# Attention and gated-MLP gradients on one core: where dV^T, dK^T, K^T and V^T are turned

## The chip, the core and the metric

The kernel runs on one core of a Trainium2 chip. The metric is the device time of one execution in microseconds (us). The engines named below are TensorE (PE, with its weight loads PEld), VectorE (DVE), ScalarE (ACT), GpSimd (POOL) and SyncE (SP). Here SP issues the DMA transposes, which turn 2-byte data on the way through the crossbar into SBUF, and POOL issues nearly all plain DMAs. Each of the two has one in-order queue of instructions, and the transfers of both run on the same 16 DMA engines. In the profile the transfers issued by SP are q1 ("hardware_dynamic") and those issued by POOL are q0 ("software_dynamic").

## The reference, cut to what matters

The forward pass and the gradients of eight of its inputs are computed, in bf16, with S = 2048 rows, D = 576, H = 32 heads of Dh = 128 (so HD = 4096) and F = 4608:

```
xn = layernorm(x)
q  = xn @ wq                              # per head [2048, 128]
p  = softmax(q k^T / sqrt(128))           # per head [2048, 2048]
s  = concat_heads(p v) @ wo
g  = silu((sigmoid(xn @ w_gate) * (xn @ w_up)) @ w_down)
out = x + s * g
grads of x, k_cache, v_cache, wq, wo, w_gate, w_up, w_down for a given grad_out
```

Two of the gradients matter here: out_2 is dK and out_3 is dV, both [32, 2048, 128], 512 KB for each head.

## The kernel before, in words

The work goes through stages. The times are those of the profiled execution.

1. **MLP forward** (to about 485 us): g, u, the products with w_down, and the gradient that enters attention. At its end K^T of head 0 is made by PE transposes (`prep_kt`, line 553).
2. **Attention** (about 485 to 3615 us): 32 heads. A head has 32 *slots*, one for each of its 16 query tiles in phase 1 and one for each in phase 2. Phase 1 (`main1`, line 640) makes the scores of one query tile, [128, 2048], on PE (line 631), ACT takes the exponential into a bf16 *slab* (line 649), and SP turns the slab by DMA transpose (`transpose_slab`, line 625) into a tile of the pool `wpt`, named PT. Phase 2 (`main2`, line 697) makes dP on PE (line 701), ACT and DVE make dS in the same slab (lines 704 to 708), and SP turns it again (dST). Five slots (`SKEW`) after its slab was made, `tail1` or `tail2` multiplies the turned slab with V or K (line 678), 16 matmuls for each slab.
3. **Output projection** (to about 3764 us, lines 905 to 962): needs all heads' outputs from scratch, turned by `load_oT` (line 582).
4. **MLP weight gradients** (about 3764 to 4339 us, lines 1010 to 1066): 18 blocks of 256 columns. A block has 16 `dh` products with their DVE and ACT work, and then six accumulations over 16 row tiles (`accumulate`, line 977): two for d w_down, two for d w_up, two for d w_gate. The last four are turned by SP (line 1063). Loads of the next block, stores of du and dg, and stores of gradients go through POOL.
5. **Attention weight gradients** (about 4339 to 4590 us, lines 1102 to 1127): eight groups of four heads. A head has one accumulation for d wo and one for d wq, which SP turns (line 1120). At a group's start POOL issues the 2 MB loads `load_on` and `load_dq` for the next group. After every second head SP also turns one of ten pieces of w_up and w_gate (128 x 4608, `load_T_rows`, line 63) for the last stage.
6. **dx** (to the end): accumulations over 104 blocks (line 1159), fed by DMA transposes (line 1098).

Within attention, the heads' side work is laid out by `plan` (line 784): `put(slot, cols, fn)` hangs a piece of work into a slot, with its cost in PE columns. The four pieces that matter:

- `prep_kt` (line 795): 16 PE transposes of K of the *next* head in slot 12 of phase 2 (`NTH + 4`), through PSUM, with two ACT copies of 128 x 1024 (line 40).
- `prep_vt` (line 807): 16 PE transposes of V in slot 11 of phase 1, with two DVE copies (line 42). Both go through `pe_transpose_blocks` (line 146).
- `Partial` for dV^T: two halves over the query tiles. The second half ends in slot 7 of phase 2 and writes its sum, [128, 2048], into the buffer of K^T, which is free by then (line 749). Then SP turns that buffer into the tile `kvn` (line 752) and POOL stores it to out_3 (line 753).
- `Partial` for dK^T: the same, one phase later. It ends in slot 7 of the next head's phase 1, uses the buffer of V^T, and goes to out_2.

K^T and V^T of the next use may be written only when those buffers are free again. In attention the order of the instructions on each engine is made by the framework's scheduler from this program order and the dependencies. In stages 3 to 6 the order on SP and POOL is the program's own (`manual_schedule`, line 881).

Of the kernel before, what the change touches and what calls it, by code (L numbers as in the profile page):

```python
# [13 lines left out]
P = 128  # L14
# [52 lines left out]
def kernel(  # L67
# [41 lines left out]
    gd_d = dram.tile([2, P], f32, name="gd_d")  # L109
    on2_d = dram.tile([S, HD], bf, name="on2_d")  # L110
    dq2_d = dram.tile([S, HD], bf, name="dq2_d")

    pers = ctx.enter_context(tc.tile_pool(name="pers", bufs=1))
    ident = pers.tile([P, P], bf, name="ident")
# [476 lines left out]
    def attention(fast):  # L591
        with ExitStack() as es:
# [1 line left out]
                return es.enter_context(tc.tile_pool(name=("f_" if fast else "g_") + name, bufs=bufs, **kw))  # L594
            slabp = pool("slab", SLABS)
            wsneg = None if fast else pool("wsneg", 3)
            wpt = pool("wpt", 7 if fast else 4)
            wt, stg = pool("wt", 2), pool("stg", 2)
            stat, hstat = pool("stat", 8), pool("hstat", 2)
            ps_big = pool("ps_big", 2, space=PSUM)  # L600
# [7 lines left out]
            acc_box[0] = acc_alloc  # L608
            warm = stat.tile([P, 1], f32, name="warm")
            nc.scalar.activation(warm[:], eps_t[:], AF.Exp)  # L610

            def start_head(h):
                hs = heads_pre[h] if h == 0 else new_head(h)
# [107 lines left out]

            class Partial:

                def __init__(self, hs, lo, hi, nat, part, turned, out_dram, eng, factor=1.0):
                    self.lo, self.hi, self.nat, self.factor = lo, hi, nat, factor
                    self.part = part[:].rearrange("p t d -> p (t d)")
                    self.turned, self.out_dram, self.eng = turned, out_dram, eng
                    self.n = 0
                    self.slabs = hs.slabs

                def step(self):
                    chunk, j = divmod(self.n, SUB)
                    self.n += 1
                    cs = slice(chunk * CH, (chunk + 1) * CH)
                    if j == 0:
                        self.acc = acc_tile()[:].rearrange("p a b -> p (a b)")[:, :CH]
                    m = self.hi - self.lo
                    for qt in range(self.lo + m * j // SUB, self.lo + m * (j + 1) // SUB):
                        nc.tensor.matmul(self.acc, lhsT=self.nat[:, qt, :], rhs=self.slabs[qt][:, cs],  # L739
                                         start=(qt == self.lo), stop=(qt == self.hi - 1))  # L740
                    if j < SUB - 1:
                        return
                    if self.out_dram is None:
                        if self.factor == 1.0:
                            alt.copy(self.part[:, cs], self.acc, eng=self.eng)
                        else:
                            alt.scaled(self.part[:, cs], self.acc, self.factor, eng=self.eng)
                        return
                    nc.vector.scalar_tensor_tensor(self.turned[:, cs], self.acc, self.factor, self.part[:, cs], op0=ALU.mult, op1=ALU.add)
                    if chunk == NCH - 1:  # L750
                        kvn = stg.tile([P, NT, P], bf, name="kvn", bufs=1)
                        nc.sync.dma_start_transpose(kvn[:], self.turned)
                        nc.gpsimd.dma_start(self.out_dram.rearrange("(p t) d -> p t d", t=NT), kvn[:])

            def part_tile():
                return stg.tile([P, NT, P], f32, name="part", tag="part", bufs=1)
# [27 lines left out]
            def plan(h):  # L784
                b1, b2 = 2 * NT * h, 2 * NT * h + NT
                hd = lambda: heads[h]
                pl = b2 - 2 * NT if h else None
                if h:
                    put(pl, 0, lambda: heads.__setitem__(h, start_head(h)))
                    for c in range(4):  # L790
                        put(pl + q(c), 0, lambda c=c: load_k(hd(), c, 4))
                        put(pl + q(skew + 3 + c), 0, lambda c=c: load_v(hd(), c, 4))
                    put(pl + q(4), 0, lambda: load_wo(hd()))
                    put(pl + q(5), 0, lambda: load_wq(hd()))
                    put(pl + q(NTH + 4), NT * P, lambda: prep_kt(hd()))
                    put(pl + q(skew + 4), DT * P, lambda: prep_wot(hd()))
                    for sc in range(NSC):
                        put(pl + q(skew + 4 + 2 * sc), DT * CH, lambda sc=sc: prep_qt(hd(), sc))
                for qt in range(NT):
                    put(b1 + qt + skew, NT * P // 2, lambda qt=qt: tail1(hd(), qt, 0))  # L800
                    put(b1 + qt + skew, NT * P // 2, lambda qt=qt: tail1(hd(), qt, 1))
                for sc in range(NSC):
                    put(b1 + q(sc), DT * CH, lambda sc=sc: prep_dot(hd(), sc))
                    put(b1 + q(sc + 1), nb * P, lambda sc=sc: prep_don(hd(), sc))
                for qt in range(NT):
                    put(b1 + max(qt + 1, q(2 + qt // nb)), 0, lambda qt=qt: scale_don(hd(), qt))
                put(b1 + q(NTH + 3), NT * P, lambda: prep_vt(hd()))
                put(b1 + q(NTH + 2), NT * P, lambda: prep_qn(hd()))
                for qt in range(NT):
                    put(max(b1 + qt + 1, b1 + NT - 4 + qt // 2 if qt < NTH else b1 + NT + qt), 0, lambda qt=qt: scale_qn(hd(), qt))  # L810
                put(b2 + 1, 0, lambda: post1(hd()))
                parts = {}

                def first(key, rhs, lo, hi, eng, factor=1.0):
                    parts[key] = part_tile()
                    return Partial(hd(), lo, hi, rhs, parts[key], None, None, eng, factor)
                spread(b1 + NTH, lambda: first("v", hd().dOn, 0, NTH, "v"))
                spread(b2, lambda: Partial(hd(), NTH, NT, hd().dOn, parts["v"], hd().KT, out_3[0, h], None))
                spread(b2 + NTH, lambda: first("k", hd().Qn, 0, NTH, "s", SCALE))
                spread(b2 + NT, lambda: Partial(hd(), NTH, NT, hd().Qn, parts["k"], VT[:], out_2[0, h], None, SCALE))  # L820
                for qt in range(NT):
                    put(b2 + qt + skew, NT * P // 2, lambda qt=qt: tail2(hd(), qt, 0))
                    put(b2 + qt + skew, NT * P // 2, lambda qt=qt: tail2(hd(), qt, 1))
# [56 lines left out]
    with late("pc") as pc, late("pcw") as pcw, late("pcf") as pcf, \  # L880
# [126 lines left out]
        def load_dq(dq_, hg):  # L1007
            nc.gpsimd.dma_start(dq_, rows_view(dq2_d, hg * HG * P, HG * P))

        with late("b1r", 2) as dblk, late("b1l") as ldp, late("b1t", 3) as tmpp, late("b1o", 2) as outp, \  # L1010
                late("b1ps", 4, space=PSUM) as ps, late("b1pa", 2, space=PSUM) as psa:
            ah1 = ldp.tile([P, 2, NT, FB], bf, name="ah1")
# [3 lines left out]
            for fb in range(NFB):  # L1016
# [11 lines left out]
                if fb == NFB - 1:  # L1028
                    if NFB % 2:
                        dqb0_late = True  # L1030
                    else:
                        dqb0_late = False
                        load_dq(dqb0, 0)
                for st in range(NT):
                    srows = slice(st * P, (st + 1) * P)
                    dh = ps.tile([P, FB], f32, name="dh")
# [11 lines left out]
                if fb == NFB - 1:  # L1048
                    nc.gpsimd.dma_start(ds_all, rows_view(ds_d, 0, D))
                    load_on(onb0, 0)  # L1050
                for fl in range(FB // P):
                    dwd = outp.tile([P, D], bf, name="dwd")
                    accumulate(psa, h_blk, doB, slice(fl * P, (fl + 1) * P), dwd, "acc")
                    r0 = fb * FB + fl * P
                    nc.gpsimd.dma_start(out_8[r0:r0 + P, :], dwd[:])
                for (blk_, out_, nm) in ((du_blk, out_7, "dwu"), (dg_blk, out_6, "dwg")):
                    stg_ = outp.tile([P, DT, FB], bf, name=nm)
                    for fl in range(FB // P):
# [43 lines left out]
        with late("c2w") as wp, late("c2b") as blk, late("c2s", 2) as sb, late("c2ps", 4, space=PSUM) as ps:  # L1102
# [3 lines left out]
            for hg in range(NHG):  # L1106
# [6 lines left out]
                for hl in range(HG):  # L1113
                    h = hg * HG + hl
                    lcols = slice(hl * P, (hl + 1) * P)
                    dwo = sb.tile([P, D], bf, name="dwo")
                    accumulate(ps, onb, ds_all, lcols, dwo, "acc")
                    nc.gpsimd.dma_start(out_5[h * P:(h + 1) * P, :], dwo[:])
                    accumulate(ps, dqb, xn_all, lcols, dqTs[h % 2], "acc")
                    nc.sync.dma_start_transpose(dwq[:, :, lcols], dqTs[h % 2][:])  # L1120
                    if h % gap == gap - 1 and wT_pieces:
                        load_T_rows(nc, *wT_pieces.pop(0))
                    if hg == NHG - 1 and hl < len(cf_pre) and NHG % 2 == 0:
                        chunks[hl] = load_chunk(hl)
                store_T(out_4, cols, dwq)
            while wT_pieces:
                load_T_rows(nc, *wT_pieces.pop(0))

        with late("c4s", 2) as sb, late("c4cf") as chp, late("c4ps", 2, space=PSUM) as ps:
            wqT_sb = wd_flat[:, :H * D].rearrange("p (h d) -> p h d", d=D)  # L1130
# [104 lines left out]
```

## Time and profile before

| what | us |
|---|---|
| median of 9 runs | 5011.94 (5004.31 to 5024.34) |
| profiled execution | 5016.16 |
| its span | 5014.4 |
| PE busy | 4899.3 (98%) |
| DVE busy, ACT busy | 2574.7, 2573.5 (51% each) |
| crossbar queue q1: share of 16 DMA engines' span | 76.9% for 732.94 MB |
| plain queue q0: the same | 20.2% for 323.04 MB |
| `kvn` stores, 512 KB each: issue to landing, median | 5.2, 64 times |
| PT and dST transposes, 512 KB each: issue to landing, median | 4.8 and 5.1, 512 times each |

A busy PE is one whose matmuls follow each other; a matmul's own duration (219 ns for 128 columns) is longer than the pitch at which such matmuls follow, since they are pipelined. The share of a DMA queue counts the time that its packets took, so it can pass 100% when packets of two transfers overlap on an engine.

### The profile page before, as it was taken

The numbers are of one execution on the slowest core, as the hardware profiler recorded it, in microseconds if no ns is written. First come the engines' busy times: TensorE is split into PE (matmuls) and PEld (weight loads), VectorE is DVE, ScalarE is ACT, GpSimd is POOL, SyncE is SP. The second block draws the span as 40 slices with busy tenths as digits, with TensorE's granted clock in tenths as the row PEclk, the third lists the DMA queues.
The fourth block names the chain that finished last, engine by engine and source line by source line (L and its number), as shares of the span: only waits on it lengthen the run. The fifth ranks groups of instructions, "written<-read, shape, count | busy, mean of one in ns | idle before, by whom it ended". The sixth has DMA issues, their size and how long they took to land.

```text
span 5014.4 us, 103423 instructions
## 1 busy us (share of the span) xinstructions
PE 4899.3 (98%) x41454; PEld 2960.1 (59%) x42192; DVE 2574.7 (51%) x6721; ACT 2573.5 (51%) x4637; POOL 854.4 (17%) x1315
## 2 busy tenths in 40 slices
PE   8999999999999999999999999999799999999999
PEld 4445666666666666666666666666446666554554
DVE  4544665666666666666656656665434444100111
ACT  4422766766766676676677667666313333211000
POOL 3322111111111111111111111111122222211000
PEclk9999999999999999999999999999999999999999
DMA  7886999999999999999999999999996665797976
GB/s 259 273 206 169 220 219 221 221 218 228 215 215 224 217 225 216 230 211 227 229 214 225 222 219 223 225 219 217 199 202 207 196 191 188 226 261 169 172 139 122
DMA packets 2892753, 1063.35 MB, mean 212 GB/s; under 512 B 2795425, under 2 KB 2799650, under 8 KB 2892258
## 3 DMA queue, kind: packets, MB, share of 16 engines
q1 hardware_dynamic: 2792866, 732.94, 76.9%
q0 software_dynamic: 98784, 323.04, 20.2%
q8 instruction: 332, 5.44, 0.5%
q14 instruction: 163, 1.34, 0.1%
q10 hardware_dynamic: 608, 0.59, 0.0%
HBM read 175.31 MB, written 182.13 MB: 71 GB/s over the span
## 4 chain that ended last, share of the span: by engine, by line
PE 92%; DMA 4%; issue 2%; DVE 1%; SPq 0%; POOL 0%; ACT 0%; POOLq 0%; ACTq 0%; DVEq 0%
PE acc L678 18%; PE acc L739 18%; PE acc L977 13%; PE sp L631 8%; PE dp L701 8%; PE acc L1159 7%; PE acc L213 5%; PE u_ps L448 3%; PE g_ps L446 3%; PE dh L1038 3%; PE acc L531 2%; PE acct L146 2%; PE acc L947 2%; DMA dST<-Pq 1%; DMA KQ<-on_d 1%
## 5 line engine op out<-in xcount | busy, mean ns | idle before, releaser
L649 ACT ACTIVATE Pq<-sp 128x1024 bf16<-128x1024 f32 x1024 | 1047.0, 1024 | 316.5 <-PE sp L631 245.0
L704 DVE SCALAR_TENSOR_TENSOR Pq<-dp,negdelta,Pq 128x1024 bf16<-128x1024 f32 x512 | 654.8, 1279 | 37.9 <-PE dp L701 37.2
L707 ACT ACTIVATE t<-dp,negdelta 128x1024 bf16<-128x1024 f32 x512 | 567.6, 1115 | 174.5 <-PE dp L701 158.5
L678 PEld LDWEIGHTS <-dST 128*128 128x128 bf16 x8192 | 510.7, 98 | 170.6 <-DMA dST<-Pq 22.7
L678 PEld LDWEIGHTS <-PT 128*128 128x128 bf16 x8192 | 501.2, 98 | 139.7 <-DMA PT<-Pq 18.2
L678 PE MATMUL acc<-Kn,dST 128*128 128x128 bf16 x8192 | 562.3, 219 | 19.3 <-DMA dST<-Pq 17.7
L631 PE MATMUL sp<-KQ 128*128 128x512 bf16 x1858 | 568.7, 380 | 2.2 <-ACT Pq L649 2.1
L701 PE MATMUL dp<-VT,dOT 128*128 128x512 bf16 x1859 | 569.3, 379 | 0.2
L678 PE MATMUL acc<-Vn,PT 128*128 128x128 bf16 x8192 | 542.7, 219 | 18.1 <-DMA PT<-Pq 16.2
L708 DVE TENSOR_TENSOR Pq<-t,Pq 128x1024 bf16<-128x1024 bf16 x512 | 354.5, 692 | 364.7 <-ACT t L707 357.9
L739 PE MATMUL acc<-Pq,dOn 128*128 128x512 bf16 x1982 | 528.3, 379 | 10.1
L739 PE MATMUL acc<-Pq,Qn 128*128 128x512 bf16 x2013 | 523.8, 380 | 8.2
L719 ACT ACTIVATE dq_n<-acc,rsc 128x128 bf16<-128x128 f32 x512 | 188.1, 367 | 347.4 <-PE acc L678 347.4
L1176 DVE SCALAR_TENSOR_TENSOR junk<-acc,xn_all 128x512 f32<-128x512 f32 (+1 forms) x32 | 13.9, 452 | 640.5 <-ACT dxn L1175 640.5
L739 PEld LDWEIGHTS <-Qn 128*128 128x128 bf16 x2048 | 200.4, 98 | 240.9 <-issue 1.3
L739 PEld LDWEIGHTS <-dOn 128*128 128x128 bf16 x2048 | 199.1, 98 | 234.5 <-issue 1.1
L631 PEld LDWEIGHTS <-KQ 128*128 128x128 bf16 x2048 | 179.4, 98 | 124.5 <-issue 3.9
L701 PEld LDWEIGHTS <-dOT 128*128 128x128 bf16 x2048 | 177.9, 98 | 110.4 <-issue 1.8
L672 POOL DMA_DIRECT2D on_d<-o_n x128 | 96.9, 757 | 801.4 <-DVE junk L690 449.7
L1040 DVE TENSOR_TENSOR du_blk<-dh,ah 128x256 bf16<-128x256 f32 x288 | 120.3, 418 | 194.6 <-PE dh L1038 192.6
L1175 ACT ACTIVATE dxn<-acc 128x512 f32<-128x512 f32 (+1 forms) x32 | 12.8, 406 | 400.5 <-PE acc L1159 393.0
L50 DVE TENSOR_SCALAR o_n<-acc,rinv_all 128x128 bf16<-128x128 f32 x352 | 123.2, 350 | 171.1 <-PE acc L678 162.0
(215 smaller groups left out, 6958.2 us busy)
## 6 DMA issues: line engine op xcount, KB each, us to landing
out_dram<-kvn POOLq DMA_DIRECT2D x64, 512.0 KB, 5.2
ah<-a_d POOLq DMA_DIRECT2D x18, 1024.0 KB, 7.0
ah<-h_d POOLq DMA_DIRECT2D x18, 1024.0 KB, 9.5
du_d<-du_blk POOLq DMA_DIRECT2D x18, 1024.0 KB, 8.3
dg_d<-dg_blk POOLq DMA_DIRECT2D x18, 1024.0 KB, 9.9
h_d<-h_row POOLq DMA_DIRECT2D x64, 256.0 KB, 3.3
a_d<-a_row POOLq DMA_DIRECT2D x64, 256.0 KB, 3.6
x_all<-in_A_k_cache_dram SPq DMA_DIRECT2D x64, 256.0 KB, 3.6
```

Of the source, the lines that this page charges most:

```text
L213: nc.tensor.matmul(av[:, :CH], lhsT=w[:, i, :], rhs=srcT[:, i, cs], start=(i == 0), stop=(i == DT - 1))
L631: nc.tensor.matmul(sp[:, c * CH:(c + 1) * CH], lhsT=hs.QT[:, qt * P:(qt + 1) * P], rhs=hs.KT[:, hf * HW_ + c * CH: hf * HW_ + (c + 1) * CH ...
L649: nc.scalar.activation(Pq[:, hsl], sp[:], AF.Exp, scale=SCALE, accum_out=hs.rsp[:, hf:hf + 1])
L678: nc.tensor.matmul(hs.acc[:, 0, :], lhsT=T[:, kt, :], rhs=rhs[:, kt, :], start=(kt == 0), stop=(kt == NT - 1))
L701: nc.tensor.matmul(dp[:, c * CH:(c + 1) * CH], lhsT=hs.dOT[:, qt * P:(qt + 1) * P], rhs=hs.VT[:, hf * HW_ + c * CH: hf * HW_ + (c + 1) * C ...
L704: nc.vector.scalar_tensor_tensor(Pq[:, hsl], dp[:], hs.negdelta[:, qt:qt + 1], Pq[:, hsl], op0=ALU.add, op1=ALU.mult)
L707: nc.scalar.activation(t[:], dp[:], AF.Identity, bias=hs.negdelta[:, qt:qt + 1], scale=1.0)
L708: nc.vector.tensor_tensor(Pq[:, hsl], t[:], Pq[:, hsl], op=ALU.mult)
L719: nc.scalar.activation(hs.dq_n[:, qt % G4, :], hs.acc[:, 0, :], AF.Copy, scale=hs.rsc[:, qt:qt + 1])
L739: nc.tensor.matmul(self.acc, lhsT=self.nat[:, qt, :], rhs=self.slabs[qt][:, cs], start=(qt == self.lo), stop=(qt == self.hi - 1))
L977: nc.tensor.matmul(accs[j][:, :nn], lhsT=lhs[:, st, cols], rhs=rhs[:, st, n0:n0 + nn], start=(st == 0), stop=(st == NT - 1))
L1159: nc.tensor.matmul(self.accs[sl][j][:, :nn], lhsT=ch[:, kk, sl * P:(sl + 1) * P], rhs=wT[:, k0 + kk, n0:n0 + nn], start=(self.k + kk == 0) ...
```

## The change

K^T of heads 1 to 31 and V^T of all heads are no longer made on PE. SP turns the loaded K or V, [128, 16, 128], into the buffer of K^T or V^T by one DMA transpose (`turn_nat`), K in slot 11 of phase 2 and V in slot 11 of phase 1. dV^T and dK^T are no longer turned in attention. POOL stores them as they are, [128, 2048] for each head, to a scratch tensor `kvT_d`. The scratch is turned later: `kv_turn` (SP) turns one [128, 2048] block from scratch into a tile, and `kv_store` (POOL) stores that tile to out_2 or out_3. There are 64 such blocks. Each of the 18 blocks of stage 4 takes two, and each head of stage 5 takes one until none is left (28 heads). The pool `wpt` of turned slabs has 8 buffers, not 7, and the tile `kvn` of attention is gone.

```diff
+    kvT_d = dram.tile([H, 2, P, S], bf, name="kvT_d")
...
-            wpt = pool("wpt", 7 if fast else 4)
+            wpt = pool("wpt", 8 if fast else 4)
...
+            def turn_nat(dst, src):
+                nc.sync.dma_start_transpose(dst[:].rearrange("p (t q) -> p t q", q=P), src[:].rearrange("p t d -> p (t d)"))
...
                     nc.vector.scalar_tensor_tensor(self.turned[:, cs], self.acc, self.factor, self.part[:, cs], op0=ALU.mult, op1=ALU.add)
                     if chunk == NCH - 1:
-                        kvn = stg.tile([P, NT, P], bf, name="kvn", bufs=1)
-                        nc.sync.dma_start_transpose(kvn[:], self.turned)
-                        nc.gpsimd.dma_start(self.out_dram.rearrange("(p t) d -> p t d", t=NT), kvn[:])
+                        nc.gpsimd.dma_start(self.out_T, self.turned)
...
-                    put(pl + q(NTH + 4), NT * P, lambda: prep_kt(hd()))
+                    put(pl + q(NTH + 3), 0, lambda: turn_nat(hd().KT, hd().Kn))
...
-                put(b1 + q(NTH + 3), NT * P, lambda: prep_vt(hd()))
+                put(b1 + q(NTH + 3), 0, lambda: turn_nat(hd().VT, hd().Vn))
...
+        kv_left = [(h, k) for h in range(H) for k in (1, 0)]
+        kv_wait = []
+
+        def kv_turn(pool):
+            if kv_left:
+                h, k = kv_left.pop(0)
+                t_ = pool.tile([P, NT, P], bf, name="kvn", bufs=2)
+                nc.sync.dma_start_transpose(t_[:], kvT_d[h, k])
+                kv_wait.append((t_, (out_2, out_3)[k][0, h]))
+
+        def kv_store():
+            if kv_wait:
+                t_, dst = kv_wait.pop(0)
+                nc.gpsimd.dma_start(dst.rearrange("(p t) d -> p t d", t=NT), t_[:])
...
+                kv_turn(ldp)
                 for st in range(NT):
...
                     load_on(onb0, 0)
+                kv_store()
+                kv_turn(ldp)
                 for fl in range(FB // P):
                     dwd = outp.tile([P, D], bf, name="dwd")
...
                     nc.gpsimd.dma_start(out_8[r0:r0 + P, :], dwd[:])
+                kv_store()
...
                     lcols = slice(hl * P, (hl + 1) * P)
+                    kv_turn(blk)
                     dwo = sb.tile([P, D], bf, name="dwo")
...
                     nc.sync.dma_start_transpose(dwq[:, :, lcols], dqTs[h % 2][:])
+                    kv_store()
...
+            while kv_left or kv_wait:
+                kv_turn(blk)
+                kv_store()
```

## The prediction

> **What bounds the kernel now.** I read the page first: PE is busy 98% of the span, and 92% of the chain that ended last is PE. So time is won where PE instructions go, and lost where PE begins to wait. Next I read the windows, cut at the stages. Columns: start and end, length, busy time of PE, PEld, DVE, ACT and POOL with instructions, granted PE clock, DMA share, GB/s.
>
> ```profile
> 485.00:3615.00 3130.00, 3068.40 (x27567) 1965.39 (x28046) 1985.33 (x5248) 2130.92 (x3579) 449.72 (x725) 1.00 1.11 220
> ...
> 3764.00:4339.00 575.00, 568.80 (x4752) 352.54 (x4823) 257.54 (x836) 181.87 (x495) 150.80 (x180) 1.00 0.64 197
> 4339.00:4500.00 161.00, 159.59 (x1289) 82.78 (x1314) 0.00 (x0) 28.33 (x82) 31.50 (x46) 1.00 0.91 254
> 4500.00:4590.00 90.00, 89.27 (x723) 46.36 (x736) 0.00 (x0) 16.00 (x46) 14.34 (x21) 1.00 0.60 174
> ```
>
> PE is full in attention (first line) and in both weight-gradient stages. DVE and ACT have a third of attention free. The DMA engines do not: their share is 1.11 in attention, 0.64 in the MLP gradients, 0.91 and 0.60 in the two parts of the attention gradients. The waits of PE say whether that high share hurts; here they are for 600 to 3450 us (total, times, longest):
>
> ```profile
> PE acc L678 <- DMA dST<-Pq: 5.3, 4, 2.9
> PE acc L678 <- DMA PT<-Pq: 2.7, 2, 1.9
> ```
>
> In 2850 us PE waits 8 us for turned slabs. Attention is PE's, with DMA close behind.
>
> **Part 1: the PE transposes go.** The timeline of PE around one V batch (start, length):
>
> ```profile
> 1579.45 1.06 PE L678 MATMUL acc<-Vn,PT 128*128 128x128 bf16 x16
> 1580.34 1.06 PE L146 MATMUL acct<-ident,Vn 128*128 128x128 bf16 x16
> 1581.24 0.38 PE L631 MATMUL sp<-KQ 128*128 128x512 bf16 x1
> ```
>
> The lengths overlap, so I count from start to next start: 1581.24 - 1580.34 = 0.90 us for 16 transposes, 56 ns each. The K batch (1533.18 to 1534.08) gives 0.90 too. 31 K and 32 V batches go: 63 x 0.90 = **-56.7 us**. PE has no gap before or after them, so all of it counts if nothing else is late. The copies that go with them I price at nothing: 62 on ACT (59.7 us) and 64 on DVE (41.0 us) lie on engines with slack, where PE did not wait for them.
>
> The pages would put this otherwise. The Trainium skill, "VectorE: DVE Perf Modes", The three transpose paths, has 390 ns for a 128x128 transpose on TensorE and 1309 ns on the crossbar, and its rules prefer TensorE when PSUM will do. By 390 ns the gain would be 63 x 16 x 0.39 = 393 us, and by 1309 ns one slab would take 21 us. Here PE pitches them at 56 ns and the crossbar turns a 16-block slab every 2.62 us, so neither figure prices a stream.
>
> **Part 2: attention's transfers.** SP turned 64 `kvn` tiles and now turns 63 K and V tiles of the same size, also from SBUF; POOL stores 64 x 512 KB as before. The work on the DMA engines stays, in a head that shrinks from some 95 to 93.2 us, so the share goes from 1.11 to about 1.13. Is that room? Ten-microsecond windows:
>
> ```profile
> 1510.00:1520.00 10.00, 9.95 (x91) 6.33 (x91) 8.65 (x11) 5.55 (x7) 1.18 (x2) 1.00 1.35 273
> 1550.00:1560.00 10.00, 9.95 (x82) 5.88 (x81) 4.63 (x16) 6.67 (x13) 0.00 (x0) 1.00 0.64 145
> 3640.00:3650.00 10.00, 6.07 (x26) 2.63 (x27) 3.61 (x5) 0.00 (x0) 4.28 (x8) 0.51 1.19 185
> 4600.00:4610.00 10.00, 6.69 (x54) 3.30 (x54) 0.00 (x0) 0.00 (x0) 0.00 (x0) 0.95 1.16 112
> ```
>
> In the first, the share is 1.35 and PE does not wait; in the second, where slots carry projections, it falls to 0.64, so a queue drains there. I price it at 0 (bounds: -8 us, if the eighth buffer removes the waits above, and +57 us, if DMA keeps the old pace of a head).
>
> New are two waits on SP. The K turn writes the buffer that POOL now stores from, and so waits for that store, which waits for DVE's last sum. Behind it on SP queue the slab transposes, and PE waits for those. Before, the `kvn` transpose was issued at 1521.27, as soon as that sum was there. A store issued then lands some 5.2 us later (the `kvn` stores' median) plus 0.55 us of issue: 1527. The K batch stood at 1533, and one slot (2.62 us) earlier is 1530.5: the store is done 3.5 us before. For V: 1571.8 + 5.75 = 1577.5 against 1580.3. In the planned places no wait falls due, and both tiles land (5.5 us) about 12 us before first use. Cost 0, upper bound under rival C.
>
> **Part 3: MLP gradients.** Each of 18 blocks (32.3 us) gets two turns and two stores. A turn of 128x2048 from DRAM is not in the trace. Rates: in 4339 to 4500 us the queues stand at
>
> ```profile
> q0 software_dynamic: 7168, 26.87, 47.5%
> q1 hardware_dynamic: 54717, 13.77, 43.2%
> ```
>
> (packets, MB, share): 2.85 us of all engines per plain MB and 5.05 per turned MB. Bounds for 0.524 MB turned: 1.49 us at the plain rate, 3.8 us (half of the fastest landing, 7.6, of a 1 MB `on_d` transpose). I take 0.524 x 5.05 = 2.65, and 1.49 for a store: 4.14 us a tile. A block's share goes from 0.64 to (20.6 + 8.3)/32.3 = 0.90. SP is idle from 3985.5 to 4002.2 in a block, which takes both turns; the next a/h loads land 16 us before use (3803 against 3819.6); the stores before `dwd` and `dwu` on POOL find their tiles landed. Cost 0; in a pile-up, those 16 us would have to go first.
>
> At the last block the loads for the next stage already end 2.1 us late (PE on `wdT_sb<-on_d`, landing 20.8 us). Two stores now lie among them: 2 x 1.49 = **+3 us** (0 if they drain behind the loads, 8.3 if both tiles' whole work comes first).
>
> **Part 4: attention gradients.** Here is the bill. 28 heads of 7.84 us get a turn on SP, ahead of that head's `dqT` transpose, and a store on POOL, ahead of the next head's store and the next group's loads. Heads 0 to 19 also carry the w_up and w_gate pieces. Work until 4500: 161 x 0.91 = 146.5, plus 20 x 4.14 = 82.8, together 229.3 us of all engines in 161 us, a share of 1.42. What can the engines do? The two windows above in which PE waits for a turned load show 1.19 and 1.16; attention's peak is 1.35. At 1.16 the stretch needs 198 us (+37), at 1.35 170 us (+9). I take 1.2, by the waiting windows: 191, +30. Some is absorbed: `dqT` has two buffers, 15.7 us, of which landing takes 6.3, so PE sees a delay from about 9.4 us on. **+20 us** (0 to 28). The last 12 heads need 54 + 33 = 87 of 90 us: no loss, little recovery. A waiting PE also loses clock (0.51 in the window at 3640): +3 us (0 to 10).
>
> A rule would make this cheaper: the Trainium skill, "Advanced Engine Details and Errata", X-Bar Transpose (TRN2), says transposes run as fast as plain DMAs. The queue lines above contradict it, 5.05 against 2.85 us/MB. By the rule a tile costs 2.98 us, the stretch 206/1.2 = 172 us, the loss some 2 us, and the sum would be 4965 beside the profiled 5016.
>
> **Sum.** -56.7 + 0 + 3 + 20 + 3 = -30.7 us. From the profiled execution's 5016.16: 4985.5. That execution is 4.2 us above the median of the runs, 5011.94, so beside the median I forecast **4981 us**.
>
> **Rivals.**
> - *A, forecast*: attention gives 57 us, the attention gradients take back some 20 to 35. 4970 to 4998. Chance 0.42.
> - *B, the transfers hide*: packets overlap better than in the waiting windows (1.35 is seen with PE running), the last heads take up the rest. 5011.9 - 56.7 = 4955, less up to 8. Chance 0.26. For it: the piece-laden windows reach 359 GB/s without a wait. Against: that is with loads, not turns.
> - *C, slower: SP blocked in attention.* The scheduler may issue a turn right behind its store; it does hoist (the `xnT<-on_d` transpose stands at 3514, its place in the program is after phase 2 of the last head). SP then stands still up to 5.75 us. A dST slab has 4 slots, 10.5 us, less its landing of 5.0 to 7.4: 3.1 to 5.5 us of slack. From 3.1 us of blocking on PE waits; at 5.75 it is 2.6 us a turn, 63 x 2.6 = 164 us: 5012 - 57 + 164 + 26 = 5145, and half of that wait still ends at 5063. For it: POOL already waits 10 us for some loads, and a store queued there comes later still. Against: the margins of part 2. Chance 0.14.
> - *D, the attention gradients pay in full*: share 1.16, no slack, 37 + 8 + 10: 5010; 4998 to 5022. Chance 0.12.
> - *E, the change does not do what it says*: DMA sets the pace of a head, 95 us stay, and the late stages are paid on top: 5012 + 26 = 5038. For it: 1.11 in attention. Against: landings there stay at 4 to 7 us and do not grow. Chance 0.06.
>
> **How the numbers follow.** The likeliest case is A. B's fast end is 4947; D ends at 5022. From 4948 to 5020 lie A, B and most of D: 0.79. A measurement tells about 0.2%, 10 us, from no change. Faster (below 5002): A, B and little of D, 0.69. Same (5002 to 5022): the rest of D and the mild end of C, 0.13. Slower: C and E, 0.18.
>
> **What would show it.** No `ident,Kn` or `ident,Vn` on PE in attention, and heads of about 93.2 us: part 1. PE waits on PT and dST still near 8 us: part 2; tens of microseconds, with long waits of SP for a store, would mean C. The 18 blocks still at 32.3 us: part 3. Heads of the attention gradients at 8.6 to 9 us instead of 7.84 until about head 20, with PE waiting for `on_d`, `dq_d` or PSUM behind `dqT`: part 4; 7.84 would mean B. A turn that takes the engines far from 2.65 us makes part 4 wrong.

## The result: the changed kernel is slower

| | before | after |
|---|---|---|
| median, us | 5011.94 (31 runs, 5003.00 to 5025.26) | 5072.01 (10 runs, 5048.79 to 5094.43) |
| span of the profiled execution, us | 5014.4 | 5072.7 |

The ratio is 1.0117, 95% interval 1.0102 to 1.0132: 1.2% slower. The forecast was 4981 us, with a range of 4948 to 5020. Medians and ratios here and below are of fast executions; a slow one of e3 (5151.74 us) is not counted.

I cut both traces where the first matmul of each stage starts. Stage lengths in us, with the DMA share of the stage. They are of one profiled execution each, and whole executions of the changed kernel lie up to 46 us apart, so a difference of 10 or 20 us between two runs' stages is not clear of noise by itself.

| stage | before | after | difference |
|---|---|---|---|
| attention | 3128.0 (1.11) | 3065.8 (1.13) | -62.2 |
| output projection | 141.9 | 135.0 | -6.9 |
| MLP weight gradients | 584.8 (0.63) | 619.3 (1.09) | +34.5 |
| attention weight gradients | 250.8 (0.80) | 345.6 (1.07) | +94.8 |
| dx | 425.7 | 423.8 | -1.9 |

Attention gave about what was forecast. The two stages that took the turns over lost 129 us, where the forecast had 26.

The windows of the changed kernel, with the columns of the prediction's windows: attention, the MLP gradients, then the attention gradients' first 161 us and their rest.

```profile
485.00:3549.00 3064.00, 3009.55 (x26529) 1906.91 (x27007) 1952.35 (x5184) 2079.35 (x3517) 451.34 (x725) 1.00 1.13 225
3684.00:4303.00 619.00, 585.99 (x4831) 361.94 (x4901) 267.89 (x867) 186.99 (x508) 174.62 (x224) 0.98 1.09 245
4303.00:4464.00 161.00, 128.56 (x1003) 66.03 (x1025) 0.00 (x0) 19.23 (x56) 29.69 (x45) 0.92 1.10 267
4464.00:4649.00 185.00, 135.40 (x1005) 68.29 (x1025) 0.00 (x0) 23.86 (x70) 31.26 (x49) 0.85 1.05 238
```

In the first line PE is 58.8 us less busy than before; some of that is PE records that the two traces lack (1038 instructions fewer, where 63 x 16 = 1008 went). e1 and e3 below, whose counts of matmuls and weight loads agree, put the fall at 50. In the other lines the DMA share stands at 1.05 to 1.10 and PE is no longer full; its clock falls to 0.85. PE's waits over the whole changed kernel (total, times, longest):

```profile
PE acc L979 <- ACT dwo L40: 79.5, 6, 23.9
PE dh L1056 <- ACT ndh L1060: 26.8, 8, 11.5
PE acc L682 <- DMA dST<-Pq: 17.4, 13, 5.7
...
PE acc L682 <- DMA PT<-Pq: 8.8, 5, 5.9
```

The last two, on attention's turned slabs, were 17.7 and 16.2 us before, so attention has no new wait. (Of the output projection's 6.9 us, 4.4 are a shorter wait for its first load, `KQ<-on_d`, 7.9 before and 3.5 after.) The first two are new (0 and 0.7 us before). The first is in the attention gradients. ACT has 19 and 24 us of work in their two windows, so it is not the bound; it waits too, for stores (`dwo` has two buffers). POOL, which issues the stores, waits there for the turn on SP:

```profile
ACT dwo L40 <- DMA out_dram<-dwo: 244.3, 28, 31.0
POOL out_dram L1025 <- DMA kvn<-kvT_d: 255.0, 27, 22.1
```

The queues of the changed kernel from 4303 to 4464 us (packets, MB, share), against the lines of 161 us in the prediction:

```profile
q1 hardware_dynamic: 61308, 15.43, 60.7%
q0 software_dynamic: 7345, 27.37, 49.0%
```

As much as before passed in the same 161 us (15.43 MB turned against 13.77, 27.37 plain against 26.87), although more was wanted. The turned MB now takes 6.33 us of all engines, where it took 5.05.

**Where the MLP gradients wait.** SP and POOL of the changed kernel around a block that loses time (start, length, instruction; in brackets the idle time before it and what ended it):

```profile
3893.45 11.41 SPq L1019 DMA_TRANSPOSE kvn<-kvT_d  x1
3904.98 10.49 SPq L1084 DMA_TRANSPOSE dwu<-dwT  x2
3915.57 4.62 SPq L1084 DMA_TRANSPOSE dwg<-dwT  x2
3920.28 3.10 SPq L1019 DMA_TRANSPOSE kvn<-kvT_d  x1
```

```profile
3919.29 0.54 POOL L1025 DMA_DIRECT2D out_dram<-kvn  x1 [20.07 <-DMA kvn<-kvT_d]
3921.85 0.76 POOL L987 DMA_DIRECT2D out_dram<-dwu  x1 [2.02 <-DMA dwu<-dwT]
...
3926.55 1.20 POOL L895 DMA_DIRECT2D ah<-a_d  x1
3927.75 1.16 POOL L895 DMA_DIRECT2D ah<-h_d  x1
```

The block's second turn holds SP for 11.41 us, the `dwT` transposes come after it, and POOL stands 20.07 us in front of the turned tile. The next block's a and h are issued only at 3926 and 3927; the chain of the work that ended last has `ah<-h_d` for 25.98 us from 3927.75, then DVE, then PE. Two theories fit. **Placement**: the turn stands where POOL's 4 MB (a, h, du, dg) are in flight; the same turn elsewhere would be free. **Work**: turns and stores are more than the DMA engines have room for, wherever they lie.

### The profile page after: what moved, and what is told of

It is laid out like the page before. It is cut to its first block, busy times and chain, and to the rows that moved or that the text cites. A ratio compares the mean times of both kernels' runs of the same rounds, so it can differ in the third digit from the quotient of the medians.

```text
span 5072.7 us, 101580 instructions
## 1 busy us (share of the span) xinstructions
PE 4863.4 (96%) x40447; PEld 2909.1 (57%) x41184; DVE 2541.6 (50%) x6657; ACT 2521.2 (50%) x4575; POOL 891.1 (18%) x1379
## 4 chain that ended last, share of the span: by engine, by line
PE 83%; DMA 8%; issue 3%; SPq 3%; DVE 1%; POOL 0%; ACT 0%; POOLq 0%; ACTq 0%; DVEq 0%
PE acc L682 18%; PE acc L743 17%; PE sp L635 8%; PE dp L705 8%; PE acc L979 7%; PE acc L1185 6%; PE acc L214 5%; PE u_ps L449 3%; PE g_ps L447 3%; PE acc L532 3%; DMA ah<-h_d 3%; PE acc L949 2%; PE dh L1056 2%; PE acct L147 1%; SPq L1019 1%
## 5 line engine op out<-in xcount | busy, mean ns | idle before, releaser
L682 PEld LDWEIGHTS <-dST 128*128 128x128 bf16 x8192 | 508.2, 98 | 164.4 <-DMA dST<-Pq 25.2
L743 PEld LDWEIGHTS <-Qn 128*128 128x128 bf16 x2048 | 200.5, 98 | 241.6 <-issue 2.4
L1057 DVE SCALAR_TENSOR_TENSOR nbl<-ah 128x256 bf16<-128x256 bf16 x288 | 98.7, 417 | 261.9 <-DMA ah<-h_d 251.3
```

Source lines behind the costliest of these rows:

```text
L682: nc.tensor.matmul(hs.acc[:, 0, :], lhsT=T[:, kt, :], rhs=rhs[:, kt, :], start=(kt == 0), stop=(kt == NT - 1))
```

## The experiments

Ratios are to the kernel before, with the 95% interval. "MLP" and "attn" are the lengths of the two weight-gradient stages.

| run | median us | ratio | attention | MLP | attn | dx |
|---|---|---|---|---|---|---|
| e1 no late turns, no late stores | 4945.69 | 0.9875 (0.9854 to 0.9896) | 3066 | 585 | 251 | 423 |
| e2 all turned in attention | 5156.86 | 1.0299 (1.0274 to 1.0324) | 3265 | 584 | 251 | 422 |
| e3 late part alone | 5099.28 | 1.0176 (1.0094 to 1.0259) | 3100 | 622 | 337 | 424 |
| e4 store one tile later | 5052.84 | 1.0092 (1.0065 to 1.0119) | 3064 | 617 | 320 | 424 |
| e5 plain load for the turn | 5018.51 | 1.0023 (1.0007 to 1.0039) | 3062 | 585 | 346 | 423 |
| e6 no late stores | 4988.02 | 0.9957 (0.9940 to 0.9974) | 3071 | 618 | 276 | 421 |
| e7 quiet half of the block | 5048.21 | 1.0073 (1.0051 to 1.0095) | 3070 | 585 | 360 | 424 |
| e8 three a block | 5011.12 | 1.0001 (0.9990 to 1.0012) | 3068 | 643 | 257 | 432 |
| e9 store that never waits | 5069.72 | 1.0107 (1.0073 to 1.0141) | 3063 | 624 | 328 | 423 |
| e10 three quiet places | 5027.79 | 1.0023 (1.0008 to 1.0038) | 3056 | 584 | 266 | 499 |
| e12 none in a group's first head | 5022.52 | 1.0021 (1.0001 to 1.0040) | 3062 | 584 | 300 | 438 |
| e13 46 tiles late | 4969.23 | 0.9921 (0.9895 to 0.9946) | 3087 | 583 | 253 | 424 |
| e14 as e10, stores by SP in dx | 4956.01 | 0.9891 (0.9862 to 0.9919) | 3064 | 584 | 254 | 431 |
| e15 late stores alone | 4955.59 | 0.9895 (0.9864 to 0.9925) | 3058 | 584 | 264 | 425 |

### The parts alone: e1, e2, e3

e1 stores dV^T and dK^T straight into the outputs, unturned:

```diff
...
-        kv_left = [(h, k) for h in range(H) for k in (1, 0)]
+        kv_left = []
```

> The changed kernel without any late turn and late store: dV^T and dK^T go from attention straight into out_3 and out_2, unturned, so the turning of these two gradients is left out. Theory W (work): the late stages lose because the 16 DMA engines cannot move more in them, about 250 GB/s, in whatever order. Theory Q (queues): they lose because a turn from scratch becomes slow beside POOL's bulk transfers, and because POOL, in order, waits for it with a store ahead of the next loads and stores. Both expect the same here: attention 3066 us from its first score to the first matmul of the output projection (before: 3128), MLP gradients back from 619 to 585 us, attention gradients back from 346 to 251 us, together 4940 to 4952 us. More than 4965 would mean that part of the loss of the changed kernel sits elsewhere.

e2 is the kernel before with K^T and V^T by crossbar:

```diff
-put(pl + q(NTH + 4), NT * P, lambda: prep_kt(hd()))
+put(pl + q(NTH + 3), 0, lambda: turn_nat(hd().KT, hd().Kn))
-put(b1 + q(NTH + 3), NT * P, lambda: prep_vt(hd()))
+put(b1 + q(NTH + 3), 0, lambda: turn_nat(hd().VT, hd().Vn))
```

> The kernel before with K^T and V^T by crossbar and nothing else: dV and dK are still turned and stored in attention. Attention then has 63 transposes of 512 KB more than before, 2.8 us of all engines each by its queue share. If attention's DMA has room (share 1.13 to 1.19), it is as fast as the changed kernel's attention, 3066 us, the late stages are as before, and the kernel takes 4942 to 4956 us. If the engines are full at 1.13, attention stretches by 1.19/1.13 to some 3230 us and the kernel takes about 5115 us. In between: PE waits on PT and dST grow from 26 us.

e3 is the changed kernel with the two `put` lines of the kernel before.

> The changed kernel with K^T and V^T on PE as before, so that only the late turning is left of the change. Both theories: attention as before, 3128 us (up to 8 us less, since SP has 64 transposes fewer), and the late loss in full, 35 + 95 us: 5130 to 5145 us. If the late loss comes out much smaller, it depended on how attention ended.

e1 puts the loss wholly into the two late stages: without their extra transfers both have the lengths of before, and the time is 1.25% below it. e2 shows that attention has no room for all four: with the crossbar turning K, V, dK and dV it takes 199 us more than e1's, some 3.1 us for each of 64 turns more (e2 has seven slab buffers, e1 eight). Its windows line (attention) and its waits of PE:

```profile
483.00:3748.00 3265.00, 3093.36 (x27015) 1926.85 (x27014) 1953.33 (x5185) 2078.28 (x3518) 451.19 (x727) 0.98 1.13 221
```

```profile
PE acc L681 <- DMA dST<-Pq: 90.6, 35, 10.3
PE acc L681 <- DMA PT<-Pq: 76.1, 31, 5.6
```

The share is 1.13 here too, the same as in the changed kernel: it doesn't rise further, the stage gets longer. e3 is 28 us shorter in attention than before, at a share of 1.03, though PE still turns K and V: PE's waits for turned slabs are 10.1 us where they were 33.9. The attention lines of e3 and e1 differ by PE's batches:

```profile
483.00:3583.00 3100.00, 3087.30 (x28026) 1963.22 (x28025) 1985.47 (x5249) 2132.96 (x3580) 452.82 (x727) 1.00 1.03 212
483.00:3549.00 3066.00, 3037.23 (x27016) 1905.84 (x27015) 1953.40 (x5185) 2079.69 (x3518) 452.81 (x727) 1.00 1.13 225
```

PE's busy time falls by 50 us, but with 63 turns back on the crossbar the waits grow again (26.2 us in the changed kernel), and the stage gains 34. From before to the changed kernel, then, some 50 of the 62 us are PE's batches and 8 are shorter waits for slabs; the rest is not attributed.

### The MLP gradients: e4 to e8

e4 has three `kvn` buffers in the MLP gradients and, in both stages, stores a tile when the next has been turned; e6 leaves all late stores but the last out.

```diff
...
-            if kv_wait:
+            if len(kv_wait) > (1 if kv_left else 0):
...
```

> The changed kernel with each late store issued one tile later on POOL (three buffers for the tile in the MLP gradients, two in the attention gradients), so that POOL no longer waits for the turn that SP has just issued. Same work, same bytes. Theory W: 5060 to 5085 us, as the changed kernel. Theory Q: the 413 us in which POOL waits for the turns mostly go, the MLP gradients come back to 585 to 595 us, and the attention gradients, where SP is still held up by slow turns, to 280 to 310 us: 4980 to 5015 us.

```diff
-                nc.gpsimd.dma_start(dst.rearrange(...), t_[:])
+                if not kv_left and not kv_wait:
+                    nc.gpsimd.dma_start(dst.rearrange(...), t_[:])
```

> The changed kernel with all late turns but without the 64 late stores, except the last (out_2 and out_3 are left out). It takes 33 MB from POOL's queue and also every wait of POOL for a turn. Theory W: 1.49 us of engines for each store, 54 us in the MLP and 42 us in the attention gradients, a loss of some 10 and 60 us left: 590 to 605 and 300 to 315 us, total 5005 to 5030. Theory Q: what is left is SP, held up by slow turns ahead of the weight gradients' own transposes: 585 to 600 and 265 to 290 us, total 4970 to 5000.

Neither helps the MLP gradients (617 and 618 us): POOL's wait for the turned tile and the store's bytes are not the cause there. In e4 POOL waits for the `dwu` transposes that stand behind the turn on SP instead, 283.6 us where it was 140.2. e5 loads the tile unturned in the same place, on the same queue:

```diff
-                nc.sync.dma_start_transpose(t_[:], kvT_d[h, k])
+                nc.sync.dma_start(t_[:].rearrange("p t d -> p (t d)"), kvT_d[h, k])
```

> The changed kernel with each late turn replaced by a plain DMA of the same 512 KB from scratch into the same tile, on the same queue (SP) at the same place; the late turning is left out, so out_2 and out_3 hold unturned data. Theory W (the engines are full, a crossbar MB costs 5.05 and a plain MB 2.85 us): 28 x 1.16 us less in the attention gradients and 36 x 1.16 us less in the MLP gradients, at most 30 and 20 us of time: 346 becomes 315 to 320, 619 becomes 600 to 610, total 5025 to 5045. Theory Q (a crossbar transfer is starved beside POOL's bulk transfers, which a plain one is not): tiles land in 5 to 8 us instead of up to 34, POOL does not wait long, 585 to 590 and 270 to 290 us, total 4965 to 4995.

e7 keeps the turns, but issues a block's two between the `d w_up` transposes, and the stores behind the next block's `dwd` stores:

```diff
+        QUIET = (("dwu", 0), ("dwu", 1))
...
-                kv_turn(ldp)
                 for st in range(NT):
...
-                kv_store()
-                kv_turn(ldp)
                 for fl in range(FB // P):
...
-                kv_store()
+                while kv_wait:
+                    kv_store()
...
                         nc.sync.dma_start_transpose(stg_[:, :, lcols], dwT[:])
+                        if (nm, fl) in QUIET:
+                            kv_turn(ldp)
...
```

> The changed kernel with the two turns of an MLP-gradient block moved on SP from the block's start to between the d w_up transposes, where the DMA share was 0.2 to 0.4 before, and the two stores after the next block's d w_down. Attention gradients as in the changed kernel. Same work. Theory W: the MLP gradients stay at 610 to 620 us, total 5060 to 5080. Theory Q (collision with the 4 MB of loads and stores at the block's start): 585 to 592 us, total 5035 to 5045, with the attention gradients still at some 346 us.

Both bring the stage back to 585 us. It is the turn, and the turn in that place. The trace of before had said which place; these are its windows over one block, in quarters (PE's `dh` products begin at 3980.8):

```profile
3969.00:3977.00 8.00, 7.89 (x65) 4.18 (x66) 1.56 (x5) 1.40 (x4) 0.12 (x1) 1.00 0.20 49
3977.00:3985.00 8.00, 8.00 (x72) 5.73 (x70) 3.35 (x12) 3.45 (x10) 1.51 (x3) 1.00 0.37 93
3985.00:3993.00 8.00, 7.95 (x71) 5.84 (x71) 6.03 (x22) 3.97 (x11) 5.73 (x7) 1.00 0.98 256
3993.00:4001.00 8.00, 7.95 (x66) 4.08 (x66) 4.58 (x14) 1.40 (x4) 1.78 (x3) 1.00 0.99 371
```

The DMA share is 0.20 and 0.37 in one half of a block and 0.98 and 0.99 in the other. The turns stood in the full half. Their own lines in this stage, SP's time in ns (min/median/max) and the time to landing, first in the changed kernel, then in e7:

```profile
L1019 SPq DMA_TRANSPOSE kvn<-kvT_d x35: 1611/3539/16829, 3686.5 to 4273.0; - x35
...
DMA to landing us min/median/max: 4.2/8.8/33.9
```

```profile
L1020 SPq DMA_TRANSPOSE kvn<-kvT_d x34: 1600/2074/3164, 3712.1 to 4232.2; - x34
...
DMA to landing us min/median/max: 4.2/4.8/6.4
```

The median landing of a turn is 8.8 us in the full half, 4.8 in the other, and the longest 33.9 and 6.4. Over the stage, queue q1 takes 8.85 us per MB in the changed kernel (50.0% of 619 us for 34.99 MB) and 6.1 in e7 (35.2% of 586 us for 33.67 MB), against 5.6 before (15.4% of 585 us for 15.98 MB). The Trainium skill, "DMA: Bandwidth & Descriptors", section on queues, rings and completion order, says that a DMA engine takes turns between its queues packet by packet. q1's packets hold 249 bytes here (34.99 MB in 140777) and q0's 3.7 KB, so a turn beside bulk traffic would wait behind a large packet for each small one. The two prices fit this; no run varied the packet size of the traffic beside the turn, or shows that the packets of the profile are those of the page, so it isn't shown.

e8 asks how much the quiet half holds: a third turn after the first `d w_gate` transpose, and the last 10 tiles in heads 20 and later of the attention gradients.

> As the kernel with the quiet half of the block, but three turns in each MLP-gradient block (54 in all), and the last ten in heads 20 to 29 of the attention gradients, behind the w_up and w_gate pieces. Same work as the changed kernel in the two stages together. Theory W: the work only moves, the MLP gradients go to 640 us or more and the attention gradients to 255 to 265 us, total 5005 to 5020. Theory Q: both stages have room in their quiet parts, 585 to 600 and 251 to 262 us, total 4945 to 4970, the fastest kernel of the study that writes all outputs.

With three a block the stage takes 643 us, as theory W had said, and the next stage's first load is late as well (PE 16.0 us on `wdT_sb<-on_d`). But W's reason is not what the trace shows: the stage's share is 0.94, below the 1.09 of the changed kernel, and its turns land in 4.9 us (median). SP stands in front of a turn until a store frees its buffer:

```profile
SPq L1020 <- DMA out_dram<-kvn: 227.3, 16, 19.2
```

In e7 that wait is 15.8 us. No run gave e8's tiles more than their three buffers, so whether the quiet half holds a third turn is open. Ten tiles in the last heads cost 6 us (257 against 251).

### The attention gradients: e6, e9, e15, e12

e9 keeps the turns and takes the store's 512 KB from a tile that is always ready; e15 is e9 without the turns.

```diff
-  nc.gpsimd.dma_start(dst.rearrange(...), t_[:])
+  nc.gpsimd.dma_start(dst.rearrange(...), xn_all[:].rearrange("p t d -> p (t d)")[:, :NT * P])
```

> The changed kernel, but every late store has its size and its place on POOL and takes its 512 KB from a tile that is always ready (the normalized input), so that POOL never waits for a turn; what arrives in out_2 and out_3 is not dK and dV. The turns stay as they are. If the attention gradients lose by POOL's wait for a turn (255 us of waiting, ahead of the d wo stores and the next group's loads), that stage comes near the 276 us of the kernel without late stores, 276 to 300; if by the bytes of the stores, it stays at 320 to 346. The MLP gradients stay near 618 in both cases, since the slow turn on SP is still there. Time about 5000 to 5025 by the wait, 5045 to 5072 by the bytes.

> The changed kernel without the late turns, but with the late stores of 512 KB in their places on POOL, from a tile that is always ready (the normalized input); out_2 and out_3 are not dK and dV. The kernel without stores had 276 us in the attention gradients, 25 more than before, and the one with both 328 to 346. If turns and stores share one limit, the DMA engines' time, stores alone (28 x 1.49 = 42 us of work in some 50 us of room) cost little: 251 to 262. If the stores delay PE by themselves (POOL or the queue), the stage takes 290 or more. MLP gradients 584 to 590 if only the turns hurt there.

The stage's windows in e6 (turns alone), e15 (stores alone) and e9 (both, no wait of POOL for a tile):

```profile
4304.00:4580.00 276.00, 259.60 (x2045) 132.16 (x2046) 0.00 (x0) 43.19 (x126) 46.33 (x67) 0.97 1.04 261
```

```profile
4261.00:4524.00 263.00, 252.56 (x2004) 130.56 (x2044) 0.00 (x0) 43.19 (x126) 60.85 (x94) 0.98 1.00 273
```

```profile
4310.00:4638.00 328.00, 266.13 (x2008) 134.91 (x2050) 0.00 (x0) 42.61 (x126) 60.65 (x94) 0.90 1.07 264
```

Turns alone cost 25 us, stores alone 13, both together 77. Each half finds room, the two together do not: with the share at 1.07 the stage gets longer instead. My expectation for e9 that the wait is the main cause fell. With the wait on POOL the stage was another 18 us longer (328 to 346), but that is not clear of noise: e9's whole time is the changed kernel's (5069.72 and 5072.01 us), and e7, which changes only the MLP gradients, has 360 us here.

e5, with a plain load in place of the turn, takes 346 us too (its profiled execution is 17 us above its median), but not by the same waits. SP now stands 77.2 us in front of a load for its buffer (12.8 in the changed kernel); the turns that are left, those of the w_up and w_gate pieces, land in 22.2 us (14.7; 10.9 before), and the two 2 MB loads of the next group in 22.8 and 28.0 (12.8 and 17.2):

```profile
SPq L1019 <- DMA out_dram<-kvn: 77.2, 17, 12.1
```

So the plain load holds SP for only 0.32 us (median), and the loss moves to the transfers beside it; the equal length does not say that a load and a turn cost the same here.

e12, otherwise e10 below, puts no turn in a group's first head, beside which POOL loads 4 MB, and has 24 tiles in the stage:

```diff
-                    kv_turn(blk)
+                    if h % 4:
+                        kv_turn(blk)
```

> Whole computation. As the kernel with three quiet places, but in the attention gradients 24 tiles, in the second, third and fourth head of each group of four and none in the first, beside which POOL loads 4 MB; the last 4 tiles go to the dx stage. If one turn a group that meets the 4 MB is the cause (14 to 23 us on SP), the stage falls from the 346 to 360 us seen with 28 tiles to 265 to 290; if the stage pays for each tile, it stays at 251 + 24 x 3 = 323 or more. MLP gradients 585, dx 424 to 428. Time 4965 to 4990 by the first, 5020 or more by the second.

It decided nothing. The stage takes 300 us, between the two bounds, and in six of the groups one turn still holds SP for 13.1 to 14.5 us, now in the second head.

### Versions that place all or part of it: e10, e13, e14

e10 takes e7's two a block, 10 tiles in heads 20 to 29, and 18 tiles in the dx stage, one after every third chunk:

```diff
+                if n >= 15 and n % 3 == 0:
+                    while len(kv_wait) > (1 if kv_left else 0):
+                        kv_store()
+                    kv_turn(chp)
```

> Whole computation. 36 tiles between the d w_up transposes of the MLP gradients' blocks, 10 in heads 20 to 29 of the attention gradients, and 18 in the dx stage, one after every third chunk, each stored one tile later. If the loss is placement: MLP gradients 584 to 586, attention gradients 255 to 258, dx 424 to 440, in all 4945 to 4970, faster than the kernel before. If the DMA work has to be paid wherever it lies: 28 tiles by some 3 us more than the 4945 of the kernel without late turns plus its share in the other stages, 5000 or more.

Its dx stage lost 73 us, at a share of only 0.81. SP's waits there:

```profile
SPq L1122 <- PE acc L1188: 95.6, 45, 4.9
SPq L1020 <- DMA out_dram<-kvn: 93.5, 5, 25.2
```

L1020 is the turn. It waits for a store to free its buffer; that store is queued on POOL behind the stores of dx, which wait for DVE at the end of a row. The chunks for PE are queued on SP behind the turn. e14 lets SP issue these stores:

```diff
-                        kv_store()
+                        t_, dst = kv_wait.pop(0)
+                        nc.sync.dma_start(dst.rearrange("(p t) d -> p t d", t=NT), t_[:])
```

> Whole computation. The kernel with three quiet places, but in the dx stage SP issues the store of a turned tile, ahead of the next turn, in place of POOL. There, SP stood 93.5 us (5 times) in front of a turn for a tile's store that was queued on POOL behind the dx stores. If that wait was the cause of dx taking 499 us, dx comes to 425 to 445 and the time to 4950 to 4980; if the transfers themselves are, dx stays above 480 and the time at 5010 or more.

The same line in e14, and its windows line of the dx stage:

```profile
SPq L1020 <- DMA out_dram<-kvn: 47.3, 16, 4.1
```

```profile
4521.00:4952.00 431.00, 408.39 (x3261) 211.60 (x3328) 52.29 (x160) 15.00 (x66) 20.25 (x37) 0.98 0.97 197
```

The longest wait is 4.1 us in place of 25.2, and the stage takes 431 us with the same 18 tiles. e14 does the whole computation, with every transfer of the change, and is 1.1% faster than the kernel before.

e13 leaves heads 0 to 8 as before, with seven slab buffers, and moves only 46 tiles, to the places where e7 and e8 had found room:

```diff
-        kv_left = [(h, k) for h in range(H) for k in (1, 0)]
+        kv_left = [(h, k) for h in range(9, H) for k in (1, 0)]
```

> Whole computation. Heads 0 to 8 stay as in the kernel before (PE turns K and V, the crossbar turns dV^T and dK^T in attention, seven slab buffers); heads 9 to 31 are changed, and their 46 tiles go to the two places that had room: 36 between the d w_up transposes of the MLP gradients' blocks, 10 in heads 20 to 29 of the attention gradients. If the late tiles cost only where there is no room: attention 3066 + 18 x 0.9 = 3082, output projection 133 to 140, MLP gradients 585, attention gradients 255 to 266, dx 424, in all 4960 to 4980, faster than before by 0.7 to 1%. If attention's 62 us come from the eighth buffer and not from PE's batches, attention stays near 3110 and the time near 5000.

0.8% faster. Its attention keeps 18 of PE's batches and is 21 us longer than the changed kernel's, 1.2 us a batch. With seven buffers and 46 of 64 tiles moved it keeps 41 of the 62 us, where a share of 46/64 would be 45, so the eighth buffer is not what made the gain.

## Why the prediction was wrong

**Part 1, right in its mechanism, a little large in its size.** -56.7 us were forecast, and the stage is 62.2 us shorter. PE's busy time fell by 50 us (e3 to e1), 0.8 us a batch and not 0.90; that the whole came out near the forecast is partly luck, since shorter waits for slabs added 8 us, and the rest is not attributed.

**Part 2, right in size, with less room than it said.** The share came out at the forecast 1.13 and no new wait showed. But the forecast read 1.35 in one window as room. In e2 attention asked for more and the share stayed at 1.13, with 166.7 us of PE waits. The forecast's 8 us of slab waits came from a window that ends at 3450 us; another 25.7 us lay behind it. Rival C (SP blocked in attention) did not happen, and that its span, 5063 to 5145, holds the measured time is chance.

**Part 3, wrong: "SP is idle from 3985.5 to 4002.2 in a block, which takes both turns", cost 0.** It measured +34.5. SP was idle there, the DMA engines were not: their share is 0.98 and 0.99 in those microseconds. The forecast took the mean of the block, 0.64, and added the turns to it. Its sum, 0.90, is what e7 shows once the turns stand in the other half, at no cost. So the sum of work was right, and the place was not looked at. The forecast did name the 16 us by which the a and h loads are early as what a pile-up would take first; the chain shows it gone, with `ah<-h_d` landing after up to 26 us.

**Part 4, wrong in size: +20 and +3 against +94.8.** Three terms were too small.
- The price of a tile. 4.14 us were taken; the stage's DMA work rose from 200.5 us (shares of q0 and q1, 79.9% of 251) to 370.6 (107.1% of 346), 6.1 us for each of 28 tiles. Prices were read at a share of 0.91 and applied above 1.
- The capacity. 1.2 was taken; the share of the full stage is 1.07. With the forecast's own work, 200.5 + 28 x 4.14 = 316 us, that share makes 296 us, +45. So of the 75 us between +20 and +94.8 about 25 are the capacity and 50 the price. This only divides the miss: price and share are both read from the changed kernel, and their quotient is its length by construction. Nor is the price fixed: e4 moved as much in this stage (87.31 MB against 86.96) at the same share in 320 us.
- The clock. +3 was taken; PE is busy 264 us in the stage where it was 249, +15, at a clock of 0.85 to 0.92. How much of that lengthened the stage, in which PE also waits, no run shows.

The 9.4 us that "`dqT` has two buffers" was to absorb were read at the wrong tile. What ran out was `dwo`, 144 KB stores on POOL behind the turned tile; PE waited for it 79.5 us and for `dqT` not at all. What POOL's wait for the turned tile is worth is not shown (e9: 18 us in one execution's stage, 2 us in the medians of the whole).

Rival D, attention's gradients in full (5010), had the right place and too small a price; it held the MLP gradients at no cost.

What stays open: why turns and stores find room one by one and not together in the attention gradients, that is, whether the queues' packets or a bound of the engines makes the limit of 1.07 to 1.13.

## What to carry to other kernels

Read the DMA share in the microseconds into which a transfer is put, not the mean of its loop, and count what is queued behind it on its issuing engine; the same 36 turns cost 34 us in one half of a block and nothing in the other. Where the share already stands at its highest sustained value (here 1.07 to 1.13, over stages and not over 10 us), count every further transfer as time, at a price above that of a half-idle queue. When a tile is stored by a queue that waits for something else, its buffer stays taken, and the engine that fills it stops all that it feeds (e10's dx stage was 73 us longer than before, e14's, with the stores on SP, 5).

## What the runs showed of the hardware

- Where PE waited for transfers, the DMA share of the whole stage was 1.13 in attention (e2) and 1.07 to 1.09 in the attention gradients (the changed kernel, e4, e5, e7, e9 and e12): the stage got longer and the share did not rise. The share doesn't give the length, since packets took longer: the changed kernel and e4 had 1.07 with the same bytes, in 346 and 320 us.
- A turned MB took 5.1 us of all engines in the attention gradients before and 6.5 in the changed kernel's. In the MLP gradients it took 8.85 with the turns in the full half of a block and 6.1 with them in the quiet half (e7). A plain MB moved only from 2.87 to 2.95, and from 2.83 to 3.11.
- In the changed kernel a turn of 128x2048 holds SP for 1.6 to 23.2 us, and what SP issues later waits with it.
